# The last phase of a two-layer kernel: the first two pairs of token tiles interleaved

## The chip, the cores and the metric

The kernel runs on one core of one Trainium2 chip. The metric is the device time of one execution in microseconds. A timed run is one execution without the profiler, and a profiled execution leaves a trace whose span starts at the first instruction and ends at the last.

## What is computed

Retention attention over 4 batches of 576 tokens (2304 in all, 8 heads of 64) is followed by two feed-forward layers of width 512 → 2048 → 512:

```python
ret = scores * Dmat            # attention with a decay matrix, then times v
x = moe(x):   h = x @ w_in;  g = h * sigmoid(h);       x = g @ w_out
x = moe2(x):  h = x @ w_in;  r = maximum(h, 0);        out = (r * r) @ w_out
```

All inputs and outputs are float32. The change concerns only the last product, `(r * r) @ w_out` of the second layer.

## The kernel before

**Splitting.** A float32 operand is written as a high part (a cast to the matmul type, on ScalarE, called ACT in the profile: line 692) and a low part (source minus high part, on VectorE, DVE: line 693). A product of two such operands is three matmuls: high activation by high weight, high by low weight, low activation by high weight.

**Seven products for eight.** Weights and activations of the second layer are cut into 2×2 blocks, and the block product is formed from seven products of sums of blocks. Phase 1 (`product1`, line 902) makes the activations `g` and writes them to DRAM (`gD`, line 941). Phase 2 (`product2`, line 993) multiplies them with the second weight. Its work is cut into nine *pairs of token tiles* P = 0..8, each with 7 products i = 0..6. Product (P, i) is 24 matmuls of 128×256 (8 inner blocks by three), so phase 2 has 63 products.

**What product (P, i) needs.** Its weight block sum is number RF[i] of (0, 3, 1, 4, 2, 5, 6): raw data `w2r` are loaded (`load_w2`, line 885) and split into four tiles `w2s` (`split_w2`). The activations are four raw tiles `gr` a pair (`load_g`, line 954, 512 KB each, q = 0..3, also called a11, a12, a21, a22), sums of them (`sum_g`, lines 962 to 969, in four parts) and a split into `gl` (`split_g`). For i = 0 the source is raw tile 0 itself, for i = 2 raw tile 1, and for i = 1 it is the sum that part 2 (line 967) leaves behind.

**What follows product (P, i).** The even products of a pair accumulate in one PSUM bank (`pa`), the odd ones in another (`pb`). `after2` reads a bank between two products that go into it: for i = 0 ACT copies the bank (line 1001, tile `s1`), for i = 2 ACT copies it to `y` (line 1008), for the others DVE adds. Product (P, 2) adds into the bank of (P, 0) and therefore starts after the copy of line 1001. Products 5 and 6 end with an output DMA that ACT issues (line 1014).

**What sets the order.** The engines execute their instructions in the order in which the program emits them. In phase 2 the loop over n = 0..62 emits product n, then `after2` of product n − 1, and then items of a list `todo`: splits and sums with the number of the product that needs them and a cost. Up to 3.6 units of cost are emitted in each step, at most five products ahead. Loads of `gr` are emitted in steps given by the table `loads`, all on the queue of SyncE (SP). Before the loop, the weights of blocks 0, 3, 1 are split, 4 is half split, and the splits of (0, 0), (0, 1) and (0, 2) are emitted. Five loads of `w2r` (blocks 2, 5 and half of 6) and two writes of `gD` stand on SP's queue just ahead of phase 2.

Of the kernel before, what the change touches and what calls it, by code (L numbers as in the profile page):

```python
# [43 lines left out]
def kernel(  # L44
# [60 lines left out]
    first = {}  # L105
# [582 lines left out]
    def chain():  # L688
        return bank("pa"), bank("pb")

    def split(dst, src, engine=nc.vector):
        nc.scalar.copy(dst[0], src)  # L692
        low.append(lambda: engine.tensor_sub(dst[1], src, dst[0]))  # L693
# [253 lines left out]
    g_raw = {}  # L947
    g_s = {}
    g_l = {}

    def load_g(P, q, pool, tag):
        b, t = divmod(P, TT)
        r = pools[pool].tile([128, 1024], F32, tag=tag, name="gr")
        nc.sync.dma_start(out=r, in_=gD[b, t, :, q].rearrange("p m n -> p (m n)"))
        g_raw[P, q] = r
# [13 lines left out]
            nc.vector.tensor_sub(a12, a12, a11)  # L969

    def split_g(P, i, pool, engine=nc.vector):
        src = g_s[P][i]
        if pool == "w":
            parts = [wp.tile([128, 2, 512], F32R, tag="w", name="gl") for _ in range(2)]
            for e, t in enumerate(parts):
                split((t[:, 0], t[:, 1]), src[:, 512 * e : 512 * e + 512], engine)
        else:
            t = pools["ha" if n_split[0] % 6 < 4 else "hb"].tile([128, 2, 1024], F32R, tag="h", name="gl")
            n_split[0] += 1
            split((t[:, 0], t[:, 1]), src)  # L980
            parts = [t[:, :, 0:512], t[:, :, 512:1024]]
        g_l[P, i] = parts

    def product2(P, i):
        if i == 0:
            sp["y", P % 2] = {"o": chain()}
        o = sp["y", P % 2]["o"][i % 2][:, 0:256]
        for m in range(NP):
            g = g_l[P, i][m // 4][:, :, m % 4 * 128 : m % 4 * 128 + 128]
            w = w2_s[RF[i], m // 2][:, :, m % 2 * 256 : m % 2 * 256 + 256]  # L990
            for q, (lhs, rhs) in enumerate(((g[:, 0], w[:, 0]), (g[:, 0], w[:, 1]), (g[:, 1], w[:, 0]))):
                first = m == 0 and q == 0 and i in (0, 1, 4)
                mm(o, lhs, rhs, start=first, stop=m == NP - 1 and q == 2, skip_group_check=True)  # L993

    def after2(P, i):
        st = sp["y", P % 2]
        o = st["o"][i % 2][:, 0:256]
        b, t = divmod(P, TT)
        if i == 0:
            st["s1"] = pools["tq"].tile([128, 256], F32, tag="s1", name="s1", bufs=2)  # L1000
            nc.scalar.copy(st["s1"], o)
            st["y"] = [pools["tq"].tile([128, 512], F32, tag="y", name="y", bufs=4) for _ in range(2)]
        elif i in (1, 3):
            nm = "u2" if i == 1 else "u3"
            st[nm] = pools["tq"].tile([128, 256], F32, tag=nm, name=nm, bufs=2)
            nc.vector.tensor_add(st[nm], o, st["s1"])
        elif i == 2:
            nc.scalar.copy(st["y"][0][:, 0:256], o)
        else:
            h, e = ((1, 1), (1, 0), (0, 1))[i - 4]  # L1010
            nc.vector.tensor_add(st["y"][h][:, 256 * e : 256 * e + 256], o, st[("u3", "s1", "u2")[i - 4]])
            if i > 4:
                r0 = (2 * b + h) * HB + t * 128
                nc.scalar.dma_start(out=out[r0 : r0 + 128, :], in_=st["y"][h])

    def beside1(b, d, k):
# [14 lines left out]
        if b == NB2 - 1:  # L1031
            todo = {
                (1, 0): lambda: (load_w2(0, 0), load_w2(0, 1)),
                (1, 2): lambda: (load_g(0, 2, "w", "w"), load_g(0, 3, "w", "w")),
                (1, 5): lambda: (load_g(0, 0, "w", "w"), load_g(0, 1, "w", "w")),
                (1, 12): lambda: (load_w2(3, 0), sum_g(0, 0)),
                (1, 13): lambda: load_w2(3, 1),
                (2, 0): lambda: sum_g(0, 1),
                (2, 1): lambda: split_g(0, 0, "w"),
                (2, 3): lambda: sum_g(0, 2),  # L1040
                (2, 8): lambda: load_w2(1, 0),
                (2, 11): lambda: split_g(0, 1, "w", nc.gpsimd),
                (2, 12): lambda: load_w2(1, 1),
                (3, 6): lambda: load_w2(4, 0),
                (3, 7): lambda: (split_g(0, 2, "w"), load_w2(4, 1)),
                (3, 9): lambda: sum_g(0, 3),
            }
            for c, at in (
# [4 lines left out]
            ):  # L1053
                if (d, k) in at:
                    split_w2(c, at.index((d, k)), nc.gpsimd)
            if (d, k) in todo:
                todo[d, k]()
# [227 lines left out]

    todo = []
    NPP = NB2 * TT

    def need(n, cost, *emit):
        todo.append((n, cost, emit))  # L1290

    for q in (2, 3):
        need(3, 1, split_w2, 4, q)
    need(3, 0, load_w2, 6, 1)
    need(3, 1.8, split_g, 0, 3, "hl")
    for c, n in ((2, 4), (5, 5), (6, 6)):
        for q in range(4):
            need(n, 1, split_w2, c, q)
        need(n, 1.8, split_g, 0, n, "hl")
    for P in range(1, NPP):  # L1300
        n = 7 * P
        need(n, 1.8, sum_g, P, 0)
        for i in range(7):
            for part in {1: (1, 2), 6: (3,)}.get(i, ()):
                need(n + i, 1.8, sum_g, P, part)
            need(n + i, 1.8, split_g, P, i, "hl")
    loads = {}
    for P in range(1, NPP):
        for q, at in ((2, -10), (3, -10), (0, -9), (1, -8)):
            pool, tag = ("w", "w") if q == 2 and P > 1 else ("rq", "r")  # L1310
            loads.setdefault(max(7 * P + at, 0), []).append((P, q, pool, tag))

    low = []
    due = room = 0
# [1 line left out]
    def lows():  # L1316
        held = low[:]
        low.clear()
        for part in held:
            part()  # L1320

    for n in range(7 * NPP):
        if due <= n:
            lows()
        product2(*divmod(n, 7))
        if n:
            after2(*divmod(n - 1, 7))
        room = min(room, 0) + 3.6
        while todo and (room > 0 and todo[0][0] <= n + 5 or todo[0][0] <= n + 1):
            due, cost, emit = todo.pop(0)  # L1330
            if emit[0] is sum_g:
                lows()
            held = low[:]
            low.clear()
            emit[0](*emit[1:])
            for part in held:
                part()
            room -= cost
        for args in loads.pop(n, ()):
            load_g(*args)  # L1340
    after2(*divmod(7 * NPP - 1, 7))


# [54 lines left out]
```

## Time and profile before

| | us |
|---|---|
| timed runs, median of 3 (lowest, highest) | 833.56 (833.06, 838.0) |
| the profiled execution's own time | 835.54 |
| its span in the trace | 833.8 |
| phase 2 in that trace: first matmul of line 993, start of the last product | 643.40, 827.34 |

PE is TensorE, PEld its weight loads, ACT ScalarE, DVE VectorE, POOL GpSimd, SP SyncE; a name with q (SPq, ACTq) is the engine's sequencer, which issues DMAs. Times in views are microseconds from the start of the span. The granted clock PEclk is a share of 2.4 GHz. `a<-b` is written tile and read tile. A releaser behind `<-` is what ended an engine's idle time.

### The profile page before, as it was taken

Reading aid. Unit: us, or ns where it says so; the run is one execution under the profiler, and the core shown is the slowest. Engines: PE = TensorE matmul, PEld = TensorE weight load, DVE = VectorE, ACT = ScalarE, POOL = GpSimd, SP = SyncE. Lnnn points to the kernel's source line nnn. Section 1 sums busy time; section 2 is a strip of 40 time slices with the busy share of each in tenths; the row PEclk is TensorE's granted clock in tenths of the full one; section 3 lists DMA queues with packets and bytes.
Section 4 is the critical chain, followed back from the end, with each engine's and each line's share of the span. In section 5 each row is a group of like instructions: output and inputs, shape, how many; then the busy total and the mean of one; then the engine's idle time right before and its main releaser. Section 6 shows DMA issues by size and latency. Waiting matters only on the chain.

```text
span 833.8 us, 16177 instructions
## 1 busy us (share of the span) xinstructions
PE 809.6 (97%) x6410; PEld 749.4 (90%) x6410; DVE 548.7 (66%) x809; ACT 450.3 (54%) x862; POOL 187.4 (22%) x204
## 2 busy tenths in 40 slices
PE   6999989999999999999999999999999999999998
PEld 5887779999988987888887999999999999999998
DVE  5899986555334555666778566646566878777772
ACT  6777774454455445354545576645668535434430
POOL 3202003324534204223432212302254000000000
PEclk9999999999999999999999999999999999999999
DMA  9787784988534022698796375353586933444300
GB/s 354 253 249 211 254 285 142 328 313 291 191 129 154 1 88 77 213 310 316 229 308 227 122 242 167 114 177 109 160 295 202 346 139 127 144 133 138 119 26 26
DMA packets 71980, 160.70 MB, mean 193 GB/s; under 512 B 6112, under 2 KB 37344, under 8 KB 71904
## 3 DMA queue, kind: packets, MB, share of 16 engines
q1 hardware_dynamic: 67008, 150.23, 52.9%
q10 hardware_dynamic: 4896, 9.44, 3.0%
q8 instruction: 50, 0.82, 0.4%
q14 instruction: 26, 0.21, 0.1%
HBM read 104.07 MB, written 55.57 MB: 191 GB/s over the span
## 4 chain that ended last, share of the span: by engine, by line
PE 75%; DMA 4%; DVE 3%; ACT 2%; issue 1%; POOL 0%; SPq 0%; ACTq 0%; POOLq 0%; DVEq 0%
PE acc L83 15%; PE pa L902 12%; PE pa L993 11%; PE pb L902 9%; PE ph L83 9%; PE pb L993 8%; PE pa L762 4%; PE pb L762 3%; PE Q L415 2%; DMA w2c<-wt 1%; DMA w2r<-w2c 1%; DMA wr<-w 1%; PE P L364 1%; PE P L369 1%; DVE xsa L693 1%
## 5 line engine op out<-in xcount | busy, mean ns | idle before, releaser
L83 PE MATMUL ph<-xh,wi 128*128 128x384 f32 (+2 forms) x400 | 115.4, 352 | 0.8 <-ACT sg L645 0.8
L83 PE MATMUL acc<-gh,wo 128*128 128x384 f32 (+1 forms) x384 | 113.7, 357 | 0.0
L993 PE MATMUL pa<-w2s,gl 128*128 128x256 f32 x864 | 109.0, 283 | 0.9 <-DVE gl L693 0.8
L993 PEld LDWEIGHTS pa<-w2s,gl 128*128 128x128 f32 x864 | 105.9, 192 | 1.5 <-DVE gl L693 1.2
L902 PE MATMUL pa<-xa,w1s 128*128 128x384 f32 x576 | 105.9, 335 | 0.0
L902 PEld LDWEIGHTS pa<-xa,w1s 128*128 128x128 f32 x576 | 100.5, 188 | 0.1
L83 PE MATMUL acc<-gsl,wo 128*128 128x512 f32 x384 | 88.0, 390 | 0.5 <-DVE gsl L693 0.5
L692 ACT CAST gl<-gr 128x1024 fp32r<-128x1024 f32 (+1 forms) x57 | 55.9, 1003 | 59.9 <-DVE gr L967 24.5
L83 PEld LDWEIGHTS acc<-gsl,wo 128*128 128x128 f32 x384 | 71.9, 188 | 16.4 <-DVE gsl L693 0.9
L993 PE MATMUL pb<-w2s,gl 128*128 128x256 f32 x648 | 84.0, 287 | 1.6 <-ACT gl L692 0.8
L993 PEld LDWEIGHTS pb<-w2s,gl 128*128 128x128 f32 x648 | 81.2, 195 | 2.0 <-ACT gl L692 1.0
L902 PE MATMUL pb<-xa,w1s 128*128 128x384 f32 x432 | 80.9, 335 | 0.0
L83 PEld LDWEIGHTS ph<-xh,wi 128*128 128x128 f32 x400 | 73.0, 188 | 6.6 <-ACT sg L645 1.3
L83 PEld LDWEIGHTS acc<-gh,wo 128*128 128x128 f32 x384 | 70.7, 188 | 5.8
L902 PEld LDWEIGHTS pb<-xa,w1s 128*128 128x128 f32 x432 | 75.5, 188 | 0.1
L693 DVE TENSOR_TENSOR gl<-gr,gl 128x1024 fp32r<-128x1024 f32 (+1 forms) x55 | 64.7, 1181 | 13.5 <-ACT gl L692 13.4
L83 PE MATMUL ph<-xl,wi 128*128 128x384 f32 (+2 forms) x200 | 69.5, 348 | 0.0
L83 PE MATMUL acc<-gl,wo 128*128 128x384 f32 (+1 forms) x192 | 67.9, 354 | 0.0
L115 ACT ACTIVATE t<-wr 128x512 f32<-128x512 f32 x64 | 42.9, 671 | 27.6 <-DMA wr<-w 24.1
L648 DVE TENSOR_TENSOR gl<-sg,gh 128x384 fp32r<-128x384 f32 (+1 forms) x48 | 31.0, 647 | 39.8 <-ACT gh L647 39.8
L645 ACT ACTIVATE sg<-ph 128x384 f32<-128x384 f32 (+1 forms) x48 | 25.0, 521 | 52.9 <-PE ph L83 52.5
L122 DVE CUSTOM_DVE_ANT_0 t<-wr,t 128x1024 uint16<-128x1024 uint16 x64 | 47.3, 740 | 8.3 <-ACT sg L645 1.0
(140 smaller groups left out, 1333.7 us busy)
## 6 DMA issues: line engine op xcount, KB each, us to landing
wr<-w SPq DMA_DIRECT2D x64, 512.0 KB, 4.4
gD<-g SPq DMA_DIRECT2D x48, 384.0 KB, 2.6
gr<-gD SPq DMA_DIRECT2D x36, 512.0 KB, 4.7
raw<-att SPq DMA_DIRECT2D x32, 512.0 KB, 5.5
woD<-wo SPq DMA_DIRECT2D x16, 512.0 KB, 7.4
wo<-woD SPq DMA_DIRECT2D x16, 512.0 KB, 6.8
w2r<-w2c SPq DMA_DIRECT2D x14, 512.0 KB, 5.8
xq<-x SPq DMA_DIRECT2D x12, 384.0 KB, 5.5
```

Source lines behind the costliest of these rows:

```text
L83: mm(o, a, b, start=first and i == 0, stop=last and i == n - 1)
L115: nc.scalar.activation(t.bitcast(F32), hi.bitcast(F32), ACTF.Abs, scale=2.0**-112)
L122: nc.vector.tensor_tensor(t, t, lo, op=ALU.add)
L364: mm(o, dims(u, a, e, b, 768), dims(u, a, e, b, 0), start=True, stop=True)
L415: mm(w, a, b, start=e not in started, stop=last)
L645: nc.scalar.activation(s, ph, ACTF.Silu)
L648: later.append(lambda: nc.vector.tensor_sub(gl, s, gh))
L692: nc.scalar.copy(dst[0], src)
L693: low.append(lambda: engine.tensor_sub(dst[1], src, dst[0]))
L762: mm(o, lhs, rhs, start=m == 0 and i in (0, 1, 4), stop=m == 5, skip_group_check=True)
L902: mm(o, lhs, rhs, start=m == 0 and i in (0, 1, 4), stop=m == 5, skip_group_check=True)
L993: mm(o, lhs, rhs, start=first, stop=m == NP - 1 and q == 2, skip_group_check=True)
```

## The change

The products of phase 2 get a table `order2`. Before, they ran by pair: (0, 0) to (0, 6), then (1, 0) to (1, 6), and so on. Now the first fourteen run as (0,0) (0,1) (0,2) (1,0) (0,3) (1,1) (0,4) (1,2) (0,5) (1,3) (0,6) (1,4) (1,5) (1,6); from the third pair on nothing moves. The list `todo` is built in that order. Raw tiles of pair 1 are loaded in the order q = 0, 2, 3, 1 (before 2, 3, 0, 1), and loads of a step are emitted ahead of the step's `todo` items instead of behind them. The split of (1, 0) reads raw tile 0 directly, and part 0 of the sums of pair 1 is emitted with (1, 1).

```diff
     def split_g(P, i, pool, engine=nc.vector):
-        src = g_s[P][i]
+        src = g_s[P][i] if i else g_raw[P, 0]
...
+    order2 = [(0, 0), (0, 1)]
+    for i in range(7):
+        order2 += [(0, i + 2)] * (i < 5) + [(1, i)]
+    order2 += [(P, i) for P in range(2, NPP) for i in range(7)]
...
-    for q in (2, 3):
-        need(3, 1, split_w2, 4, q)
-    need(3, 0, load_w2, 6, 1)
-    need(3, 1.8, split_g, 0, 3, "hl")
...
+    for n, (P, i) in enumerate(order2):
+        if P == 0:
+            c = (None, None, None, 4, 2, 5, 6)[i]
+            for q in range(2 if i == 3 else 0, 4 if c else 0):
+                need(n, 1, split_w2, c, q)
+            if i == 3:
+                need(n, 0, load_w2, 6, 1)
+            if i > 2:
+                need(n, 1.8, split_g, 0, i, "hl")
+        else:
+            first = {0: (0,)} if P > 1 else {1: (0,)}
+            for part in first.get(i, ()) + {1: (1, 2), 6: (3,)}.get(i, ()):
+                need(n, 1.8, sum_g, P, part)
+            need(n, 1.8, split_g, P, i, "hl")
+    loads = {0: [(1, q, "rq", "r") for q in (0, 2, 3, 1)]}
...
-        product2(*divmod(n, 7))
+        product2(*order2[n])
         if n:
-            after2(*divmod(n - 1, 7))
+            after2(*order2[n - 1])
+        for args in loads.pop(n, ()):
+            load_g(*args)
...
-        for args in loads.pop(n, ()):
-            load_g(*args)
```

Two places show how instructions move. The first is ACT at the start of phase 2, right behind its last instruction of phase 1 (line 937). Before, with `w2r_6989` the second half of raw weight block 4, `gr_6600` a raw tile of pair 0 and `s1_7163` the copy of (0, 0):

```order
L937 ACTIVATE g_7036<-c_7044 128x3x128
L692 CAST w2s_7121<-w2r_6989 128x512
L692 CAST w2s_7123<-w2r_6989 128x512
L692 CAST gl_7129<-gr_6600 128x1024
L1001 COPY s1_7163<-pa_7095 128x256
L692 CAST w2s_7167<-w2r_7063 128x512
```

ACT with the change, where `gr_7121` is raw tile 0 of pair 1 and `s1_7161` the copy of (0, 0):

```order
L937 ACTIVATE g_7036<-c_7044 128x3x128
L692 CAST gl_7129<-gr_7121 128x1024
L692 CAST w2s_7131<-w2r_6989 128x512
L692 CAST w2s_7134<-w2r_6989 128x512
L1001 COPY s1_7161<-pa_7095 128x256
L692 CAST gl_7168<-gr_6600 128x1024
L1008 COPY y_7163<-pa_7095 128x256
L692 CAST gl_7228<-gr_7121 128x1024
```

The cast of (1, 0) has come to the front, ahead of the two weight casts and the copy; the cast of (0, 3) is now behind the copy.

The second place is SP's queue at the same point. Before, `gr_7131`, `gr_7133`, `gr_7135` and `gr_7137` are raw tiles 2, 3, 0 and 1 of pair 1, and `w2r_7126` is the second half of weight block 6:

```order
L885 DMA w2r_7071<-w2c_83 128x1024
L941 DMA gD_90<-g_7036 128x3x256
L941 DMA gD_90<-g_7061 128x3x256
L885 DMA w2r_7126<-w2c_83 128x1024
L954 DMA gr_7131<-gD_90 128x1024
L954 DMA gr_7133<-gD_90 128x1024
L954 DMA gr_7135<-gD_90 128x1024
L954 DMA gr_7137<-gD_90 128x1024
```

SP with the change, where `gr_7121`, `gr_7123`, `gr_7125` and `gr_7127` are raw tiles 0, 2, 3 and 1 of pair 1, and `w2r_7165` is the second half of weight block 6:

```order
L885 DMA w2r_7071<-w2c_83 128x1024
L941 DMA gD_90<-g_7036 128x3x256
L941 DMA gD_90<-g_7061 128x3x256
L954 DMA gr_7121<-gD_90 128x1024
L954 DMA gr_7123<-gD_90 128x1024
L954 DMA gr_7125<-gD_90 128x1024
L954 DMA gr_7127<-gD_90 128x1024
L885 DMA w2r_7165<-w2c_83 128x1024
```

Raw tile 0 of pair 1 has moved from the third place behind the writes of `gD`, past tiles 2 and 3, into the place that the last weight load had; that load now follows the four tiles.

## Rows read from the trace of the kernel before

**Rows 1.** The page's head and its row of busy times.

```profile
span 833.8 us, 16177 instructions
PE 809.6 (97%) x6410; PEld 749.4 (90%) x6410; DVE 548.7 (66%) x809; ACT 450.3 (54%) x862; POOL 187.4 (22%) x204
```

**Rows 2.** Timeline, PE, start of phase 2: start, duration, what [idle before <-releaser].

```profile
643.40 3.03 PE L993 MATMUL pa<-w2s,gl 128*128 128x256 f32 x24
646.26 3.04 PE L993 MATMUL pb<-w2s,gl 128*128 128x256 f32 x24
649.14 3.04 PE L993 MATMUL pa<-w2s,gl 128*128 128x256 f32 x24
652.02 3.04 PE L993 MATMUL pb<-w2s,gl 128*128 128x256 f32 x24
...
660.66 3.95 PE L993 MATMUL pa<-w2s,gl 128*128 128x256 f32 x26
665.37 2.89 PE L993 MATMUL pa<-w2s,gl 128*128 128x256 f32 x22 [0.76 <-DVE gl L693]
669.05 0.50 PE L993 MATMUL pb<-w2s,gl 128*128 128x256 f32 x2 [0.79 <-ACT gl L692]
670.31 4.40 PE L993 MATMUL pb<-w2s,gl 128*128 128x256 f32 x22 [0.76 <-DVE gl L693]
674.54 3.04 PE L993 MATMUL pa<-w2s,gl 128*128 128x256 f32 x24
```

**Rows 3.** Chain of waits, phase 2: start, duration, what.

```profile
646.32 11.30 DMA w2r<-w2c
...
657.69 1.14 ACT w2s L692 x2
658.83 0.96 ACT gl L692
...
669.03 1.24 DVE gl L693
...
674.71 2.88 PE pa L993 x24
...
827.34 2.89 PE pa L993 x24
```

**Rows 4.** Timeline, SP's queue, start of phase 2: start, duration, DMAs issued.

```profile
642.20 2.57 SPq L885 DMA_DIRECT2D w2r<-w2c  x5
644.86 1.36 SPq L941 DMA_DIRECT2D gD<-g  x2
646.32 0.57 SPq L885 DMA_DIRECT2D w2r<-w2c  x1
```

**Rows 5.** Landing of the first load of pair 1, issued 647.0 (line 954, SP).

```profile
L954 SPq DMA_DIRECT2D gr<-gD x1: 811/811/811, 647.0 to 647.0; - x1
DMA to landing us min/median/max: 11.9/11.9/11.9
```

**Rows 6.** DMA issues of the whole run: line, count, KB, median us to landing.

```profile
gr<-gD SPq DMA_DIRECT2D x36, 512.0 KB, 4.7
```

**Rows 7.** Stretches: busy time of each engine, PEclk, DMA share, GB/s.

```profile
654.00:660.00 6.00, 6.00 (x52) 6.00 (x52) 5.70 (x10) 3.88 (x6) 0.00 (x0) 1.00 1.03 414
665.00:670.00 5.00, 3.39 (x24) 2.98 (x24) 3.89 (x5) 2.05 (x3) 0.00 (x0) 1.00 0.17 66
670.00:675.00 5.00, 4.69 (x26) 4.69 (x27) 1.73 (x3) 3.05 (x4) 0.00 (x0) 0.66 0.00 0
```

**Rows 8.** Timeline, ACT: copy of (0, 0) and the cast of (1, 0).

```profile
646.47 0.37 ACT L1001 COPY s<-pa 128x256 f32<-128x256 f32 x1 [0.32 <-PE pa L993]
663.01 1.05 ACT L692 CAST gl<-gr 128x1024 fp32r<-128x1024 f32 x1 [3.22 <-DMA gr<-gD]
```

**Rows 9.** Timeline, DVE: the three sums that (1, 1) needs.

```profile
660.96 1.22 DVE L962 TENSOR_TENSOR gs<-gr 128x1024 f32<-128x1024 f32 x1
665.23 1.22 DVE L965 TENSOR_TENSOR gr<-gr 128x1024 f32<-128x1024 f32 x1
666.70 1.22 DVE L967 TENSOR_TENSOR gr<-gs,gr 128x1024 f32<-128x1024 f32 x1
```

More of the change, by code (lines that the diff above doesn't have):

```diff
@@ L1287 @@
     NPP = NB2 * TT
+    order2 = [(0, 0), (0, 1)]
+    for i in range(7):
+        order2 += [(0, i + 2)] * (i < 5) + [(1, i)]
+    order2 += [(P, i) for P in range(2, NPP) for i in range(7)]
     def need(n, cost, *emit):
         todo.append((n, cost, emit))
-    for q in (2, 3):
-        need(3, 1, split_w2, 4, q)
-    need(3, 0, load_w2, 6, 1)
-    need(3, 1.8, split_g, 0, 3, "hl")
[L1296 to L1308, printed above, removed]
+    for n, (P, i) in enumerate(order2):
[13 more added lines that the diff above has]
+    loads = {0: [(1, q, "rq", "r") for q in (0, 2, 3, 1)]}
+    for P in range(2, NPP):
         for q, at in ((2, -10), (3, -10), (0, -9), (1, -8)):
-            pool, tag = ("w", "w") if q == 2 and P > 1 else ("rq", "r")
-            loads.setdefault(max(7 * P + at, 0), []).append((P, q, pool, tag))
+            pool, tag = ("w", "w") if q == 2 else ("rq", "r")
+            loads.setdefault(7 * P + at, []).append((P, q, pool, tag))
     low = []
```

## The prediction, made before the changed kernel ran

> **What bounds the kernel now.** I read the page first: TensorE is busy 97% of the 833.8 us [rows 1], so a change pays only where TensorE stands still. Then its timeline in phase 2 [rows 2]: products start 2.88 us apart (643.40, 646.26, 649.14, 652.02), and so does the rest of the phase, 2.88 a product in the chain of waits up to the last [rows 3]. Three idle pieces, each of some 0.8 us, stand in the timeline between 660.66 and 670.31, at (1, 0) and (1, 1). Nine products at 2.88 are 25.92 us; from 643.40 they would let (1, 2) start at 669.32, and it starts at 674.54. **Phase 2 loses 5.2 us**, all of it here: from 674.54 to the start of the last product at 827.34 lie 53 products, 2.88 each. That is the most that this change can win, 0.6% of the time.
>
> Of the 5.2 us, 1.5 are clock: the last 22 matmuls of (1, 1) took 4.40 us, where 24 take 2.88, and the granted clock of 670 to 675 was 0.66, that is 1.2 GHz in part of it, after the idle pieces [rows 2, 7]. The other 3.7 us are waits. The chain shows their source [rows 3]: the last weight load, issued at 646.32, landed 11.30 us later, and behind it stood the raw tiles of pair 1, whose sums and splits end at 670.27. DVE's three sums for (1, 1) take 1.22 us each [rows 9], and the cast for (1, 0) began on ACT only at 663.01 [rows 8].
>
> Next SP's queue and the DMAs. Between 642.20 and 646.89 eight transfers are issued [rows 4]; pair 1 follows. Its first tile, issued at 647.0, landed after 11.9 us, at 658.9 [rows 5], 1.3 us behind the weight load at 657.62. The 16 DMA engines are full (share 1.03) at 414 GB/s [rows 7], and 512 KB at that rate are 1.27 us. So the loads land in the order of the queue, 1.3 us apart, and a load's landing is set by its place in that queue. By this spacing raw tile 0, third of pair 1, landed near 661.5.
>
> **The change, part by part.**
>
> 1. *Loads.* Raw tile 0 moves to the place of the weight load that landed at 657.62; the transfers ahead of it are the same. **I take its landing at 657.6.** Tiles 2, 3 and 1 follow at 658.9, 660.2 and 661.5, and the displaced weight load at 662.8, far ahead of its product, (0, 6), now the eleventh.
>
> 2. *A new wait at the head of ACT.* This decides. The cast of (1, 0) is now the first ACT instruction of phase 2, and it waits for raw tile 0. Queued behind it are the two weight casts of block 4 and the copy of (0, 0). The copy is what (0, 2) waits for, the third product, since it adds into the same bank. Before, the copy ran at 646.47 and cost nothing, under (0, 1) [rows 8]. Now, from the landing: a cast began 0.07 us after it (657.69 against 657.62 [rows 3]); two weight casts and one activation cast ended 2.10 us after that start, at 659.79 [rows 3]: the same three instructions, in another order; the copy takes 0.37 [rows 8], but consecutive ACT rows overlap by 0.1 (the casts at 657.69 last 1.14, the next is read in the chain from 658.83 to 659.79), so 0.27 to its end; TensorE began 0.04 after such a release (670.27 to 670.31 [rows 2, 3]). So (0, 2) starts at landing + 2.48 = 660.1, where it started at 649.14 [rows 2]: **11.0 us of idle TensorE**. As a formula: idle = landing − 646.7.
>
> 3. *What the stall covers.* While ACT waits it does no other split, so I check what is late next. ACT goes on with the cast of (0, 3), 1.05, until 661.1; DVE's sums start when tile 3 is there, 660.2, but behind the low parts of (1, 0), block 4 and (0, 3), so near 662.2; three sums and one addition end by 666.1, the cast of (1, 1) at 667.2 and its low part at 668.4 (1.24 [rows 3]). (1, 1) is third behind (0, 2): 660.1 + 3 × 2.88 = 668.8, and later with a slow clock. It waits for nothing, with a margin of 0.4 us or more. Block 2's four weight splits and the split of (0, 4) follow; by the same adding the low part of (0, 4) is ready near 672.3, and the product stands at 671.7 + whatever the clock costs. I put these two at nothing; what covers them is the 11 us that TensorE starts late, and if that were gone, (1, 1) would wait again as before. From the third pair on instructions and durations are the old ones.
>
> 4. *Clock.* No row shows TensorE idle for 11 us. After the idle pieces before, the clock was at its low level for part of one product, at a cost of 1.5; after the first piece alone 22 matmuls took 2.89, with the clock at 1.00 [rows 2, 7]. So the cost lies between nothing and two such stretches, 3.0; I take 1.5, the row of the longer idleness. The Trainium skill, page "TensorE: Matmul & The Clock Gate", section "Back-to-back issue gap", gives a matmul of 256 columns 213 ns at the low level; by that a product wholly at that level takes an estimated 5.1 us, 2.2 more than 2.88, and the sum below would be 0.7 us higher. No product in this trace is wholly at that level; the row's 4.40 is part of one.
>
> 5. *The rest.* The direct read of raw tile 0 and the later part 0 of the sums take away or add no instruction on any engine. The old waits go: −5.2.
>
> **Sum, against the profiled execution:** 11.0 + 1.5 − 5.2 = **+7.3 us**, 835.54 to 842.8. That execution stands 1.98 us above the median of the timed runs, 833.56, and a low stretch of 1.5 us is the one thing in this stage that may come in one run and not in another. If the timed runs lacked it, the change costs them 8.8 us. Traces of them I don't have; between +7.3 (840.9) and +8.8 (842.4) I take **+8.0: 841.6 us**. Bounds within this case: no clock cost after the change, +5.8 (839.4); two stretches after it and none before, +10.3 (843.9).
>
> **Rivals.**
>
> A. *The tile comes by its own time, not by its turn* (not slower). Over the whole run `gr` loads land in 4.7 us by the median [rows 6]; issued near 646.35, tile 0 would land at 651.05, the idle is 4.4, and the sum goes from −0.8 (no clock cost) to +0.7: near 833 us. The point is a landing at 651.9 or before, where the idle is 5.2. Against: the load in that very place needed 11.3, the next 11.9, with all engines full [rows 3, 5, 7]. For: the change issues tile 0 earlier. The Trainium skill, page "DMA: Bandwidth & Descriptors", section "Rules for kernel authors", says to issue a DMA early, compute, and wait for it late; by that rule the move is a gain. Here the issue is earlier by one place only and the wait comes far earlier, and [rows 3 to 5] speak against cover. Even with every wait of phase 2 gone, 828.3 us would be 0.6% less. 0.08.
>
> B. *Only the product that needs the tile waits.* If the copy were not held up by the cast, (0, 2) would run at 649.14, and (1, 0), fourth, would wait from 652.0 for its low part, at 657.69 + 1.05 + 1.24 = 660.0: idle 7.8 (its first two matmuls run before), +4.1 with the clock at 1.5, 837.7. For: the order on ACT is all there is against it. Against: ACT's rows run one behind the other throughout. 0.06.
>
> C. *A second wait behind the first.* The margins of (1, 1) and (0, 4) are below 1 us. If raw tile 3 or the weight casts come 2 to 3 us later than added above, TensorE idles once more and the clock falls once more: 3 us on top, 844.6. 0.08.
>
> The forecast has 0.78. Of this kernel's time 1% is 8.3 us, about what a measurement can tell from no change. The forecast's +5.8 to +10.3 lies on both sides of it: I give 0.40 of its 0.78 to under 8.3 and 0.38 above. With C at 0.07 above and the rest within, and a faster kernel only by something unseen: faster 0.02, within 1% 0.53, slower 0.45. Range 837.5 to 845.0: the forecast's own 839.4 to 843.9, B and C; left out are A and tails beyond.
>
> **What will show it.** Right: TensorE's timeline has one gap of 10 to 12 us ahead of the third product of phase 2, released by ACT line 1001; ACT's timeline shows the cast of line 692 waiting for DMA `gr<-gD` until near 657.6; the granted clock is low behind the gap; (1, 1) and (0, 4) run without a gap; phase 2 takes 7 us more from its first matmul to its last. Wrong: a gap ahead of the fourth product (B), a landing of the first `gr` load before 652 (A), or further gaps after 668 (C).

## The result and the profile after

| | before | after |
|---|---|---|
| timed runs, median of 6 each (lowest, highest), us | 834.65 (832.52, 838.03) | 842.2 (841.77, 844.25) |
| profiled execution's own time, us | 835.54 | 844.25 |
| span in the trace, us | 833.8 | 842.5 |

The ratio after to before is **1.0095, 95% interval 1.0075 to 1.0116**. The forecast was 841.6 us, slower by just under or just over 1%, and the time lies 0.6 us above it. The medians differ by 7.55 us. The highest of the six times after, 844.25, is that of the profiled execution; the other five have a median of 842.06.

TensorE's timeline at the start of phase 2 (start, duration, what, idle before and its releaser) answers to [rows 2]:

```profile
644.33 3.03 PE L993 MATMUL pa<-w2s,gl 128*128 128x256 f32 x24
647.19 3.04 PE L993 MATMUL pb<-w2s,gl 128*128 128x256 f32 x24
660.65 7.97 PE L993 MATMUL pa<-w2s,gl 128*128 128x256 f32 x48 [10.42 <-ACT s L1001]
668.46 5.92 PE L993 MATMUL pb<-w2s,gl 128*128 128x256 f32 x48
674.22 5.92 PE L993 MATMUL pa<-w2s,gl 128*128 128x256 f32 x48
```

There is one gap, where short ones stood before: ahead of the third product, (0, 2), and ACT's copy of line 1001 ends it. Two products of one bank name now follow each other, so a row has 48 matmuls. The first such row takes 7.81 us to the next, later ones 5.76.

ACT's timeline in the same stretch answers to [rows 8]:

```profile
658.25 1.04 ACT L692 CAST gl<-gr 128x1024 fp32r<-128x1024 f32 x1 [13.29 <-DMA gr<-gD]
659.20 1.13 ACT L692 CAST w2s<-w2r 128x512 fp32r<-128x512 f32 x2
660.24 0.36 ACT L1001 COPY s<-pa 128x256 f32<-128x256 f32 x1
660.50 1.04 ACT L692 CAST gl<-gr 128x1024 fp32r<-128x1024 f32 x1
```

The cast of (1, 0) waits 13.29 us for raw tile 0, then come two weight casts whose data had long been there, and then the copy, which TensorE waits for and whose bank was ready near 647.4.

The chain of waits through the gap (start, duration, what) answers to [rows 3]:

```profile
647.15 11.02 DMA gr<-gD
...
659.20 1.13 ACT w2s L692 x2
660.33 0.28 ACT s L1001
660.61 0.04 issue
660.65 7.97 PE pa L993 x48
```

The load was issued at 647.15 and landed 11.02 us later, at 658.17: nearly the 11.30 us of the weight load which stood in this place before. From the landing to TensorE's start it took 2.48 us, exactly the sum of step 2 of the prediction.

The stretches around the gap (busy time of PE, PEld, DVE, ACT, POOL, then PEclk, DMA share, GB/s) answer to [rows 7]:

```profile
650.00:660.00 10.00, 0.23 (x2) 0.03 (x1) 0.68 (x1) 1.75 (x3) 0.00 (x0) 0.74 1.04 406
660.00:665.00 5.00, 4.35 (x20) 4.35 (x21) 5.00 (x7) 1.55 (x3) 0.00 (x0) 0.50 0.59 190
665.00:670.00 5.00, 5.00 (x43) 5.00 (x42) 3.85 (x5) 3.59 (x7) 0.00 (x0) 0.99 0.52 210
```

During the gap the DMA engines are full (1.04) and everything else is nearly idle. The clock fell inside the gap, at no cost there, and was at 0.50, that is 1.2 GHz, for the first 20 matmuls behind it; from 665 on it was back.

The last row of this reading is the group of line 993 that holds the first and the last matmul of phase 2, from the list by source line:

```profile
L993 PE MATMUL pa<-w2s,gl x864: 277/283/583, 644.3 to 838.6; 128*128 128x256 f32 x173
```

From it comes a measure used below, **the loss of the phase**: last start less first start, less 181.3, which is 63 × 2.88 less one matmul's 0.12. Before it was 5.2 us (643.40 [rows 2] to 829.9, the start of the last matmul; the last product starts at 827.34 [rows 3]). After it is 13.0 us.

### The profile page after: what moved, and what is told of

Its sections match the earlier page's. It is cut to its first block, busy times and chain, and to the rows that moved or that the text cites. A ratio compares the mean times of both kernels' runs of the same rounds, so it can differ in the third digit from the quotient of the medians.

```text
span 842.5 us, 16176 instructions
## 1 busy us (share of the span) xinstructions
PE 811.0 (96%) x6410; PEld 751.1 (89%) x6410; DVE 548.9 (65%) x809; ACT 450.5 (53%) x862; POOL 186.8 (22%) x204
## 4 chain that ended last, share of the span: by engine, by line
PE 42%; DMA 3%; DVE 3%; ACT 1%; issue 1%; SPq 0%; ACTq 0%
PE pa L902 12%; PE pa L993 11%; PE pb L902 9%; PE pb L993 8%; PE acc L83 3%; DMA gr<-gD 1%; DMA wr<-w 1%; DMA w2c<-wt 1%; DVE gl L693 1%; ACT gl L692 1%; ACT w2s L692 0%; DVE gr L969 0%; DVE t L122 0%; DVE y L1011 0%; SPq L885 0%
## 5 line engine op out<-in xcount | busy, mean ns | idle before, releaser
L993 PE MATMUL pa<-w2s,gl 128*128 128x256 f32 x864 | 109.9, 286 | 10.4 <-ACT s L1001 10.4
L993 PEld LDWEIGHTS pa<-w2s,gl 128*128 128x128 f32 x864 | 107.5, 195 | 10.6 <-ACT s L1001 10.6
L993 PE MATMUL pb<-w2s,gl 128*128 128x256 f32 x648 | 82.0, 283 | 0.1
L993 PEld LDWEIGHTS pb<-w2s,gl 128*128 128x128 f32 x648 | 79.5, 192 | 0.3 <-DVE u L1006 0.3
```

## The experiments

Each ratio below is to runs of the kernel before on the same chip, with its 95% interval. The loss of the phase is from the trace of one execution of each kernel, and the timed runs need not differ by as much; where the two disagree, the text says so. Every measured time lies above the one expected of its run, in nine of the ten by 0.1 to 2.2 us and in run 5 by more. For most of them why is open; the argument goes by the traces.

**1. The cast behind the copy.**

```diff
+    first_1 = next(j for j, t in enumerate(todo) if t[2][:3] == (split_g, 1, 0))
+    todo.insert(first_1 + 4, todo.pop(first_1))
     loads = {0: [(1, q, "rq", "r") for q in (0, 2, 3, 1)]}
```

> The changed kernel, but the split of (1, 0) is listed behind that of (0, 3), so that on ACT its cast stands behind the copy of (0, 0). Loads and products are in the order of the changed kernel. Theory (the cast at the head of ACT's queue holds up the copy, and the copy holds up the third product): the copy runs near 647.4 under (0, 1), (0, 2) starts without a gap, and the gap moves to (1, 0), which has issued two matmuls when it waits for its low part: landing 658.2 + 0.08 + 1.05 + 1.24 = 660.5, against 653.2 without a wait. Idle 7.3 in place of 10.6 us, clock cost about 2 as in the changed kernel: some 3 us less than the changed kernel, near 839. Rival (the landing of the tile, not the queue on ACT, sets when TensorE goes on): the gap stays ahead of the third product or is as long ahead of the fourth, and the time stays near 842.

Measured: 840.19 us, ratio 1.0067 (1.0048 to 1.0086), loss 10.1. TensorE's timeline:

```profile
649.83 3.04 PE L993 MATMUL pa<-w2s,gl 128*128 128x256 f32 x24
659.22 0.80 PE L993 MATMUL pa<-w2s,gl 128*128 128x256 f32 x2 [6.35 <-ACT gl L692]
660.48 4.22 PE L993 MATMUL pa<-w2s,gl 128*128 128x256 f32 x22 [0.46 <-DVE gl L693]
664.54 5.92 PE L993 MATMUL pb<-w2s,gl 128*128 128x256 f32 x48
670.30 0.40 PE L993 MATMUL pa<-w2s,gl 128*128 128x256 f32 x2
671.03 5.18 PE L993 MATMUL pa<-w2s,gl 128*128 128x256 f32 x41 [0.33 <-DVE gl L693]
```

(0, 2) starts at 649.83, without a gap. Two matmuls of (1, 0) issue when its cast is done, the third when its low part is, at 660.48, near the 660.5 of the expectation. So the place of the gap in the changed kernel was made by the order on ACT. What moving the cast leaves is the wait of (1, 0) itself, whose third matmul starts 7.5 us late (660.48, where three products and two matmuls after 644.09 would have it at 652.97), and a slow product behind it (4.22 for 22 matmuls, at a granted clock of 0.65 from 660 to 665). A new piece of 0.33 us stands at (0, 4), for its low part: the margin that the prediction had put below 1 us.

**2. Three tiles ahead of the weights of blocks 5 and 6.**

```diff
-    for c, e in ((2, 0), (2, 1), (5, 0), (5, 1), (6, 0)):
+    for c, e in ((2, 0), (2, 1)):
         load_w2(c, e)
...
-                need(n, 0, load_w2, 6, 1)
+                pass
...
         for args in loads.pop(n, ()):
             load_g(*args)
+            if args[:2] == (1, 3):
+                for c, e in ((5, 0), (5, 1), (6, 0), (6, 1)):
+                    load_w2(c, e)
```

> The changed kernel, but three raw tiles of pair 1 (0, 2 and 3) are issued ahead of the four loads of raw weights of blocks 5 and 6, tile 1 behind them. ACT's order is that of the changed kernel. Theory (loads land in the order of the queue, 1.28 us apart, and the cast at the head of ACT waits for tile 0): three loads fewer stand ahead of tile 0, so it lands 3.8 us earlier, near 654.3 in place of 658.2; (0, 2) still waits for the copy, idle 6.7 in place of 10.6 us, clock cost 1 to 2: near 838. Rival (a load takes its 11 us from its issue, whatever stands ahead): tile 0, issued some 1.5 us earlier, lands 1.5 us earlier at most, and the time is 841 to 842.

Measured: 838.41 us, ratio 1.0044 (1.0025 to 1.0064), loss 9.5. The ACT row of the cast and the TensorE row behind the gap, from their two timelines:

```profile
652.45 1.04 ACT L692 CAST gl<-gr 128x1024 fp32r<-128x1024 f32 x1 [9.37 <-DMA gr<-gD]
```

```profile
654.86 8.41 PE L993 MATMUL pa<-w2s,gl 128*128 128x256 f32 x48 [6.50 <-ACT s L1001]
```

Phase 2 began at 642.45 here, so the cast began 10.0 us after it, against 13.9 in the changed kernel: 3.9 us earlier for three places, as the theory had it. The idle is 6.50, again ended by the copy. The rival, a landing counted from the issue, is out: tile 0 was issued at 645.00, 2.55 us after the start of the phase (2.82 in the changed kernel), and landed 7.4 us later in place of 11.0.

**3. Tile 0 three places later.**

```diff
+    load_w2(6, 1)
...
-                need(n, 0, load_w2, 6, 1)
+                pass
...
-    loads = {0: [(1, q, "rq", "r") for q in (0, 2, 3, 1)]}
+    loads = {0: [(1, q, "rq", "r") for q in (2, 3, 0, 1)]}
```

> The changed kernel, but its loads in the order of the kernel before: the last weight load first, then raw tiles 2, 3, 0, 1 of pair 1. Products and ACT are in the order of the changed kernel. Theory (idle is the landing of tile 0 less 647.6): tile 0 stands three places later, lands 3.8 us later, near 662.0, idle 14.4 in place of 10.6 us, time near 846. Rival (landing set from the issue): as the changed kernel, 842, since the tiles are issued within a microsecond or two of the same moment.

Measured: 848.15 us, ratio 1.016 (1.0135 to 1.0186), loss 16.5. TensorE's timeline, and the cast of (1, 0) on ACT:

```profile
646.65 3.04 PE L993 MATMUL pb<-w2s,gl 128*128 128x256 f32 x24
664.09 7.51 PE L993 MATMUL pa<-w2s,gl 128*128 128x256 f32 x48 [14.40 <-ACT s L1001]
```

```profile
661.68 1.04 ACT L692 CAST gl<-gr 128x1024 fp32r<-128x1024 f32 x1 [17.27 <-DMA gr<-gD]
```

The idle is 14.40 us, as expected; the time is 2 us above the expected 846, and the trace doesn't show why. With run 2 and the changed kernel, the idle follows the place of tile 0 in the queue over 8 us: 6.5, 10.4 and 14.4. This run alone would not tell place from issue, since tile 0 was also issued 5.4 us later after the start of the phase (652.0 less 643.78 is 8.2, against 2.8); run 2 does.

**4. Work inside the gap.**

```diff
+FILL = 84
...
+        if n == 2:
+            fill = bank("fill")
+            for _ in range(FILL):
+                mm(fill[:, 0:256], g_l[0, 0][0][:, 0, 0:128], w2_s[0, 0][:, 0, 0:256], start=True, stop=True)
         product2(*order2[n])
```

> The changed kernel with 84 matmuls of 128x256 more, into a PSUM bank that nothing reads, between the second and the third product: some 10.1 us of work inside the gap of 10.6 us. Theory (the changed kernel loses about 2 us behind the gap because the clock is granted at half): the third product still starts when ACT's copy ends, near 660.7, the granted clock stays at 1.00, the products behind the gap take 2.88 us each, and the time is 2 us below the changed kernel, near 840. Rival (the slow products behind the gap have another cause, such as operands that come late): the clock stays high, but the two products still take 7.9 us, and the time is that of the changed kernel, 842.

Measured: 841.64 us, ratio 1.0083 (1.0065 to 1.0101), loss 12.0. TensorE's timeline and two stretches (in this kernel line 993 is 994):

```profile
648.95 10.24 PE L1332 MATMUL fill<-w2s,gl 128*128 128x256 f32 x84
659.67 6.02 PE L994 MATMUL pa<-w2s,gl 128*128 128x256 f32 x48 [0.48 <-ACT s L1002]
665.52 5.92 PE L994 MATMUL pb<-w2s,gl 128*128 128x256 f32 x48
671.28 0.40 PE L994 MATMUL pa<-w2s,gl 128*128 128x256 f32 x2
672.03 4.22 PE L994 MATMUL pa<-w2s,gl 128*128 128x256 f32 x33 [0.35 <-DVE gl L694]
```

```profile
650.00:660.00 10.00, 9.52 (x79) 9.32 (x78) 1.66 (x2) 2.74 (x5) 0.00 (x0) 1.00 1.01 397
660.00:665.00 5.00, 5.00 (x44) 5.00 (x43) 4.97 (x7) 0.94 (x2) 0.00 (x0) 1.00 0.64 204
```

The clock stayed at 1.00, and the two products behind the gap took 5.85 us in place of 7.81: the 2 us were the clock's, and the rival is out. The time came back only in part. The two products end earlier, so (0, 4) now waits 0.35 us for its low part: the slow clock had covered that wait. The loss fell by 1.0 us, not 2. The intervals of this run and of the changed kernel overlap, so the timed runs alone would not show the difference.

**5. Both edits, the cast behind the copy and the tiles ahead.** The diffs are those of runs 1 and 2.

> The changed kernel with both edits of the runs before: the cast of (1, 0) behind the copy of (0, 0) on ACT, and raw tiles 0, 2, 3 of pair 1 ahead of the weights of blocks 5 and 6. Theory: what remains is the wait of (1, 0) itself. Tile 0 landed 9.95 us after the start of phase 2 in the run with the tiles ahead; cast and low part make it 12.3, and (1, 0), fourth, stands at 8.64 and issues two matmuls: idle 3.4, some 0.5 at (0, 4) or (1, 1), and 0 to 1.5 us of clock. The phase loses 4 to 5.5 us, as the kernel before did: 834 to 835. Rival (each edit takes away its own delay, and they add): 13.0 less 2.9 less 3.5 is 6.6 us, near 836.5.

Measured: 839.2 us, ratio 1.0062 (1.0038 to 1.0086), loss 8.1: neither the theory's 4 to 5.5 nor the 6.6 of two delays that add. The trace is of the fastest of the five executions (837.54); the median is 5.2 us above the kernel before, the loss 2.9. TensorE and DVE, from their timelines:

```profile
653.46 0.51 PE L993 MATMUL pa<-w2s,gl 128*128 128x256 f32 x2 [2.17 <-ACT gl L692]
657.76 4.16 PE L993 MATMUL pa<-w2s,gl 128*128 128x256 f32 x22 [3.80 <-DVE gl L693]
```

```profile
655.02 1.22 DVE L962 TENSOR_TENSOR gs<-gr 128x1024 f32<-128x1024 f32 x1 [8.06 <-DMA gr<-gD]
656.16 0.42 DVE L1006 TENSOR_TENSOR u<-pb,s 128x256 f32<-128x256 f32 x1
656.49 1.22 DVE L693 TENSOR_TENSOR gl<-gr,gl 128x1024 fp32r<-128x1024 f32 x1
```

The cast of (1, 0) ended at 653.4, but its low part began on DVE only at 656.49. In front of it stood the first sum of pair 1, waiting for tile 3. `todo` has an item fewer here than in run 1, since the last weight load is no longer listed, and "four places later" put the split behind that sum. The same fault as the change's, on another engine, made by my edit.

**6. The same with the low part ahead of the sum** (`first_1 + 3` in place of `first_1 + 4`).

> As the run with both edits, but the split of (1, 0) is listed one place earlier, ahead of the first sum of pair 1, so that on DVE its low part stands ahead of that sum, which waits for tile 3. Theory (in that run the low part was held up behind the waiting sum, 3.96 us of TensorE): the low part follows its cast, 12.3 us after the start of the phase, (1, 0) is idle 3.4 in all instead of 6.3, and the phase loses 4 to 5.5 us instead of 8.1: near 835. Rival (the low part came late for another reason): the loss stays near 8, 838.

Measured: 836.15 us, ratio 1.0015 (1.0000 to 1.0030), loss 5.5. TensorE's timeline at (1, 0):

```profile
654.02 0.50 PE L993 MATMUL pa<-w2s,gl 128*128 128x256 f32 x2 [1.76 <-ACT gl L692]
655.28 4.13 PE L993 MATMUL pa<-w2s,gl 128*128 128x256 f32 x22 [0.76 <-DVE gl L693]
```

The low part of (1, 0) follows its cast, and the loss is at the upper end of the theory's. With the order of products untouched, listing and loads alone bring the changed kernel back to about the time before.

**7. The product order alone undone.**

```diff
-    order2 = [(0, 0), (0, 1)]
-    for i in range(7):
-        order2 += [(0, i + 2)] * (i < 5) + [(1, i)]
+    order2 = [(0, i) for i in range(7)]
+    for i in range(7):
+        order2 += [(0, i + 7)] * (i < 0) + [(1, i)]
```

> The changed kernel with the product order alone undone: (0, 0) to (0, 6), then (1, 0) to (1, 6). Pair 1's raw tiles keep their new order 0, 2, 3, 1 and their place ahead of the last weight load, and the splits are listed by the product that needs them, as before. Theory (the early place of (1, 0) in the order, which puts its cast at the head of ACT, makes the gap): no gap ahead of the third product. The last weight load now lands some 19 us after the start of the phase, and the casts of block 6 and of (0, 6) stand behind it on ACT: (0, 6), seventh, waits near 5 us, (1, 1) up to 2, clock up to 1.5: the phase loses 6 to 8.5 us, 836 to 838. Rival (the new order of the loads makes the gap): a gap of 10 us ahead of the third product stays, 842.

Measured: 838.82 us, ratio 1.0050 (1.0031 to 1.0070), loss 7.4. There is no gap ahead of the third product. TensorE's timeline:

```profile
658.93 3.04 PE L993 MATMUL pb<-w2s,gl 128*128 128x256 f32 x24
665.46 0.50 PE L993 MATMUL pa<-w2s,gl 128*128 128x256 f32 x2 [3.49 <-ACT gl L692]
666.72 7.27 PE L993 MATMUL pa<-w2s,gl 128*128 128x256 f32 x46 [0.76 <-DVE gl L693]
```

The first rows from 665.46 are (0, 6), behind the casts of block 6, whose weights now come last. So the early place of (1, 0) made the gap of the changed kernel. What is left of the change (order and place of the loads, the direct read, the later first sum) loses 2.2 us more than the kernel before in the trace and 4.2 us (2.6 to 5.8) in the timed runs. Which of these three costs how much was not separated; the wait at (0, 6) is that of the displaced weights.

**8. A version by arrival.** The tiles ahead as in run 2, (1, 0) as the sixth product, and splits and sums listed by when their data land.

```diff
+    order2 = [(0, i) for i in range(5)]
+    for i in range(7):
+        order2 += [(1, i)] + [(0, i + 5)] * (i < 2)
...
+    ahead = [("w", 4), (0, 3), ("w", 2), (0, 4), (0, 5), (0, 6), (1, 0), ("s", 0), ("s", 1), ("s", 2)]
+    ahead += [("w", 5), (1, 1), ("w", 6), (1, 2), (1, 3), (1, 4), (1, 5), ("s", 3), (1, 6)]
```

Here ("w", c) are the splits of weight block c, ("s", k) is part k of the sums of pair 1, and a pair of numbers is the split of that product. The list takes the place of the one by product for pairs 0 and 1.

> A version built from the runs: tiles 0, 2, 3 of pair 1 ahead of the weights of blocks 5 and 6; products (0,0) to (0,4), then (1,0) (0,5) (1,1) (0,6) (1,2) and the rest of pair 1; and splits and sums listed by when their data land, not by the product that needs them: block 4, (0,3), block 2, (0,4), (0,5), (0,6), then (1,0) and the three sums, block 5, (1,1), block 6, and so on. Theory (the loss is the instructions that wait for a late load at the head of an engine, with ready work behind them): with 9.95 us to the landing of tile 0 and 12.5 to that of tile 3, (1, 0), sixth, stands at 14.4 us and finds its operands, (1, 1), eighth, at 20.2 and its low part near 20.4; the phase loses under 1.5 us where the kernel before lost 5.2: 830 to 831, 0.4 to 0.5% faster than before. Rival (the DMA engines, full for 20 us at the start of the phase, limit it whatever the order): a loss of 4 us or more stays, 834.

Measured: **831.71 us, ratio 0.9965 (0.9948 to 0.9983)**, loss 0.7. It beats both kernels. TensorE's timeline from (0, 4) on, and the weight casts on ACT:

```profile
657.00 5.92 PE L993 MATMUL pa<-w2s,gl 128*128 128x256 f32 x48
662.76 0.28 PE L993 MATMUL pb<-w2s,gl 128*128 128x256 f32 x1
663.46 5.90 PE L993 MATMUL pb<-w2s,gl 128*128 128x256 f32 x47 [0.42 <-DVE w2s L693]
669.20 5.92 PE L993 MATMUL pa<-w2s,gl 128*128 128x256 f32 x48
```

```profile
659.27 2.42 ACT L692 CAST w2s<-w2r 128x512 fp32r<-128x512 f32 x4 [2.26 <-DMA w2r<-w2c]
```

One piece of 0.42 us is left, (0, 5) waiting for the low part of its first weights; ACT still waits for a load (2.26 us), but with nothing ready behind it that TensorE needs. The 0.35% (0.17 to 0.52) is less than the 0.54% that a loss smaller by 4.5 us would give, which lies just outside the interval. The two traced executions differ by 2.4 us as a whole (835.54 and 833.10), since phase 2 began 2.1 us later in this one; with the same early loads it began at 642.45 in run 2.

**9. That version with its product order undone** (`order2 = [(P, i) for P in range(2) for i in range(7)]`, the list's due numbers to match).

> The version by arrival with its product order alone undone: (0, 0) to (0, 6), then (1, 0) to (1, 6); loads and the listing of splits and sums stay. Theory (interleaving is worth something here because it gives TensorE products of pair 1 while the weights of blocks 5 and 6 land late and are split behind the sums): (0, 5) stands at 14.4 us after the start and its low weights come near 17, (0, 6) waits near 1 more; the phase loses 3.5 to 5 us, 834 to 835. Rival (listing by arrival is all; the product order is worth nothing): the loss stays below 1.5 us, 831.

Measured: 836.03 us, ratio 1.0011 (0.9992 to 1.0029), loss 5.7. (0, 5) waits 2.86 us for its low weights, as expected; (0, 6) waits for nothing, but the clock falls behind the wait, and the first row after it takes 5.28 us for 23 matmuls:

```profile
661.73 5.28 PE L993 MATMUL pb<-w2s,gl 128*128 128x256 f32 x23 [2.86 <-DVE w2s L693]
```

Interleaving is worth 5 us of the loss in that version, and 3.8 us by the two ratios of the timed runs. Its benefit, which the change did not get, is real once the loads and the listing fit.

**10. That version with its loads undone** (the weights of blocks 5 and 6 ahead of the tiles again).

> The version by arrival with its loads alone undone: the weights of blocks 5 and 6 ahead of pair 1's tiles 0, 2, 3, 1, the last weight load behind them, as in the changed kernel. Theory (landing follows the place in the queue): tile 0 lands 3.8 us later, near 13.8 us after the start of the phase, and tile 3 near 16.4; (1, 0) at 14.4 waits near 2 us for its low part, and (0, 5) or (1, 1) wait behind the sums, which start 3.8 us later; the phase loses 3.5 to 5 us, 834 to 835. Rival (the place in the queue matters little once the listing is by arrival): the loss stays below 1.5 us, 831.

Measured: 835.09 us, ratio 1.0008 (0.9984 to 1.0031), loss 3.7. TensorE's timeline, (1, 0) and (0, 5):

```profile
659.78 0.50 PE L993 MATMUL pa<-w2s,gl 128*128 128x256 f32 x2 [0.45 <-ACT gl L692]
661.04 2.90 PE L993 MATMUL pa<-w2s,gl 128*128 128x256 f32 x22 [0.76 <-DVE gl L693]
663.78 0.28 PE L993 MATMUL pb<-w2s,gl 128*128 128x256 f32 x1
665.83 5.89 PE L993 MATMUL pb<-w2s,gl 128*128 128x256 f32 x47 [1.76 <-DVE w2s L693]
```

The loss is the low end of what was expected; the timed runs give no difference from before, where the trace would have it 1.5 us faster.

## Why the prediction was right

Against the profiled execution, its own terms (us):

| step | forecast | trace |
|---|---|---|
| 1, landing of tile 0 | 657.6, from a phase starting at 643.40: 14.2 after it | 658.17, from 644.33: 13.8 after it |
| 2, idle ahead of (0, 2) | 11.0 | 660.65 less 644.33 + 2 × 2.88 = 10.6 |
| 4, clock behind the gap | 1.5 (0 to 3.0) | 7.81 − 5.76 = 2.05 |
| 3, later waits | 0 | 13.0 − 10.6 − 2.05 = 0.4 |
| old waits | −5.2 | gone |
| phase 2 | **+7.3** | 13.0 − 5.2 = **+7.8** |
| before phase 2 | 0 | 644.33 − 643.40 = +0.9 |

Point by point:

- *The place of the loss* was right to the instruction: the cast waits at the head of ACT, the copy stands behind it, and the third product waits for the copy. Runs 1 and 7 each take away one side of this and the gap is gone from there.
- *Landing by place in the queue* was right. Runs 2 and 3 moved tile 0 by three places each way, and the cast began 3.9 us earlier and 4.0 later (661.68 less 643.78 is 17.9, against 13.9). Of the two, run 2 settles it, since there the issue hardly moved. Rival A is out by this, and by the 11.02 us of the changed kernel itself. The rule on issuing early and waiting late (the Trainium skill, page "DMA: Bandwidth & Descriptors", section "Rules for kernel authors") was half followed by the change, and runs 2 and 8 show what the two halves bring: with the tiles ahead alone the loss is 9.5, with the waits late as well 0.7 (run 8 also moves (1, 0) from the fourth to the sixth place).
- *Rival B*, that only the product that needs the tile waits, is what run 1 builds. Its wait, 7.8 us by the prediction, was 7.5, counted to the third matmul of (1, 0).
- *The clock* cost 2.05 where I took 1.5 out of a range to 3.0; run 4 shows that it was the clock. The 213 ns for 256 columns at the low level, by the formula in the Trainium skill (page "TensorE: Matmul & The Clock Gate", section "Back-to-back issue gap"), agree with the trace: 20 matmuls in 4.35 us of busy time at a clock of 0.50, some 0.22 us each.
- *Margins*: (1, 1) and (0, 4) waited for nothing in the changed kernel, as forecast. Their low parts were ready at 669.08 and 673.10:

```profile
667.86 1.22 DVE L693 TENSOR_TENSOR gl<-gr,gl 128x1024 fp32r<-128x1024 f32 x1 [1.11 <-ACT gl L692]
671.88 1.22 DVE L693 TENSOR_TENSOR gl<-gs,gl 128x1024 fp32r<-128x1024 f32 x1
```

That is 2.5 and 1.4 us before the third matmul of each product. Without the 2.05 us of slow clock it would be 0.4 at (1, 1), as in step 3, and a wait at (0, 4): 0.3 us of idle appear there in runs 1 and 4. That the third pair would be untouched was not quite so: a product of pair 2 waits 0.25 us at 706.15 for DVE. The rest of the 0.4 is not traced to a wait.

- *The old waits* were four pieces and not three: seen in a narrower window, (1, 0) starts at 664.11, 0.57 us after its turn (660.66 + 2.88), inside the row of 26 matmuls. The sum of 5.2 is not touched by this.
- *From 7.3 to 8.0.* The forecast added 0.7 for a low stretch that the timed runs might lack before the change. The timed runs differ by 7.55, the traced executions by 8.7. Of 55 timed runs of the kernel before that were taken beside the experiments, the 24 with a mean granted clock of 0.998 or more have a median of 833.7 us, the other 31 one of 835.55; so such a stretch comes in some executions only, but no trace shows in how many the one of phase 2 was missing.
- *Luck* is part of how near 841.6 came to 842.2. The median before turned out 1.1 us above that of the first three runs, and the difference 0.45 us below 8.0. Within the phase, 0.4 us too much for the idle stood against 0.55 and 0.4 too little for the clock and the later waits.
- *The 0.9 us ahead of phase 2* are not the change's, as far as can be told: phase 2 began between 642.45 and 645.49 us in the traces of these kernels, whose instructions ahead of it are the same or nearly so.
- *Which side of 1%* could not be told beforehand, and can't now: the interval runs from 0.75% to 1.16%. It is 0.2% wide on either side, so these runs tell differences well below the 1% that the prediction took for the least to be told.

## What to carry to other kernels

Before an early load is worth anything, look at what stands behind the instruction that waits for it: on an engine that runs in order, one cast for a tile that lands 11 us later held up a 0.36 us copy, and that copy held up TensorE. List work by when its data land, and give the products an order that keeps the ready ones in front; product order and load order each were needed for the gain of run 8 (the phase lost 0.7 us with both, 5.7 without the product order, 3.7 without the loads, and 5.2 in the kernel before; with one of them taken back, the timed runs are no faster than that kernel). The listing was not undone by itself. When the DMA engines are full, price a load by its place in the queue, not by its median time to land.

## What the runs showed of the hardware that was not expected

The clock's cost after a long stall can be hidden or bare: with fillers the granted clock stayed at 1.00 and the products behind the gap took 5.85 us in place of 7.81, but part of that went to a wait of which the slow clock had been the cover. And with the DMA engines at a share of 1.04, three loads of 512 KB fewer ahead of a tile moved the cast that waits for it by 3.9 us and three more by 4.0, about 1.3 us each in both directions, so that a landing could be worked out by counting. What the forecast did not have: a load lands in sixteen pieces, and its landing is that of a straggler. Of the weight load that landed at 657.61 in the trace of the kernel before, fifteen pieces were there between 654.90 and 656.11. Once the queue was full, the last piece came 0.8 to 1.6 us after the fifteenth in the traces of the kernel before and of the changed one, and for most loads some 0.4 us after it in run 2 and 0.75 us in run 8, and the landings stayed 1.3 us apart in all four. The cause is open.
